# Converting an output weight among the background work of an earlier stage, and storing seven block parts in pairs

## The chip, the cores and the metric

The kernel runs on one core of a Trainium2 chip. The metric is device time in microseconds (us) of one execution; lower is better. Work goes to TensorE (PE: matmuls; PEld: its weight loads), VectorE (DVE), ScalarE (ACT) and GpSimd (POOL). Every transfer between HBM and on-chip memory is issued by one queue on SyncE (SP).

## What is computed

Three blocks follow one another, for 4 batches of 768 tokens: a gated linear attention, a token and channel mixing block, and a gated feed-forward block.

```python
for t in range(S):                                   # attention, 8 heads of 48
    state = f[:, :, t, :, None] * state + einsum('bhd,bhe->bhde', k[:, :, t], v[:, :, t])
    y[:, :, t] = einsum('bhd,bhde->bhe', q[:, :, t], state)
theta = x @ w_theta                                  # mixing, x is (4, 768, 384)
y = einsum('ts,bsd->btd', w_tok_r, x * cos(theta)) + einsum('ts,bsd->btd', w_tok_i, x * sin(theta))
u = x + y
x = u + maximum(u @ w_ch, 0)
h = maximum(x @ w_in, 0)                             # feed-forward, d_ff 1024
u, v = h[..., :512], h[..., 512:]
v_n = (v - mean(v)) / sqrt(var(v) + 1e-6)
v_s = einsum('ts,bsd->btd', w_spatial, v_n) + b_spatial[None, :, None]
out = (u * v_s) @ w_out                              # w_out is (512, 384)
```

## The kernel before

The program has two stages. **Stage 1** is the attention and the mixing block of all batches, **stage 2** the feed-forward block, batch by batch.

In stage 1 PE does the attention's small products (`psc`, `pw`, `px`), the theta products (`pth`), the token mix (`acc`, 36 groups of matmuls a half batch, which read the token weights `tk` and the rotated inputs `z`), and the channel product (`hh`), which reads `uT`. `uT` is made by ACT and DVE from a finished `acc` (`p1_u`). The token weights come back from HBM for every half batch as pairs of 384 KB transfers (`tk<-tkp`) into three buffers each.

Matmuls run in a rounded format. For full accuracy an operand x is split into hi and lo (`split`): ACT writes hi, DVE writes lo = x - hi, and `mm3` does three matmuls for one product. A weight that arrives in float64 (`w_in`, `w_out`) is first made into float32 by `single`: one transfer into a staging buffer `ws` (two of them), one ACT pass, three DVE passes into `wb`. `weight` is `single` followed by `split`.

The order of instructions of stage 1 is not the order of the code. A planner (`Plan`) records every instruction with an assumed cost, runs a list scheduler over the five engines for four rounds, and pins the best order that it found on each engine. Some work of stage 2 is handed to the planner as background work, from the tick `WTICK` on and with a due time that lies `IDLE` later than the end: the conversion of `w_in` (`w2_load`, into `wi`), the split of the first batch's inputs (`p2_x`, into `x2`), and the blocks of the spatial weight (`w_blocks`). The pools `a1` and `a2` of the attention are closed before; tiles that take their place are held back by `Plan.after`.

`w_blocks` prepares what a seven-product scheme for v_s needs. For each of three row tiles s it loads two tiles of `w_spatial` into `wr`, forms four differences in `wt`, splits `wr` and `wt` as two pieces of 128x1536 through one buffer `wz` (the low part is written over its source), and stores hi and lo to HBM in `wpd0` and `wpd1`. `wr`, `wt` and `wz` exist once each, so a piece waits until the piece before has been stored.

Stage 2 does for each batch: `p2_v` (`pv`, normalised into `vr`), `p2_b` (sums of quarters of v, split into `vn`), `p2_u` (`pu`), `p2_f` (seven products `pg` with the stored blocks, read back by `p2_load` into `sp`; each is finished into the gated values `gt` by `gate`, on DVE and ACT), and `p2_o` (`po` = gt times `wo`). For batch 0 only, `p2_wo` converts `w_out` between `p2_u` and `p2_f`, four tiles of 128x384, one `weight` each.

Every instruction is recorded by one helper, so the profile gives L370 as its line; the tile names tell the places apart.

## Time and profile before

| | |
|---|---|
| median of 3 runs | 627.47 us (624.61 to 629.4) |
| profiled execution, its own time | 624.12 us |
| its span in the trace | 622.3 us |
| mean granted clock of TensorE | 0.977 of full speed |
| busy: PE, DVE, ACT, POOL | 589.8, 457.2, 333.4, 22.3 us |
| moved by DMA | 147.75 MB, 237 GB/s over the span |

Stage 1 lasts from 0 to about 372 us of the span, stage 2 from there to the end, a little under 60 us a batch in the later batches. All times of the trace are us from the start of its span. The profiled execution is a little faster than the runs that were timed.

### The profile page before, as it was taken

The numbers are of one execution on the slowest core, as the hardware profiler recorded it, in microseconds if no ns is written. First come the engines' busy times: TensorE is split into PE (matmuls) and PEld (weight loads), VectorE is DVE, ScalarE is ACT, GpSimd is POOL, SyncE is SP. The second block draws the span as 40 slices with busy tenths as digits, with TensorE's granted clock in tenths as the row PEclk, the third lists the DMA queues.
The fourth block names the chain that finished last, engine by engine and source line by source line (L and its number), as shares of the span: only waits on it lengthen the run. The fifth ranks groups of instructions, "written<-read, shape, count | busy, mean of one in ns | idle before, by whom it ended". The sixth has DMA issues, their size and how long they took to land.

```text
span 622.3 us, 14093 instructions
## 1 busy us (share of the span) xinstructions
PE 589.8 (95%) x5736; PEld 535.7 (86%) x5736; DVE 457.2 (73%) x816; ACT 333.4 (54%) x616; POOL 22.3 (4%) x54
## 2 busy tenths in 40 slices
PE   8678989999999899999999999996999999999995
PEld 8566556776898899989999998996899999999995
DVE  5776889886899649855988457896559766966681
ACT  4556675638967687834875124633453345345421
POOL 4100001000010000000000000000000000000000
PEclk9867999999999999999999999998999999999998
DMA  7798958899688888887989979897109811950332
GB/s 279 204 290 217 278 198 230 292 318 309 226 241 270 279 276 270 246 273 273 348 295 304 374 258 366 292 342 276 40 1 339 306 41 46 360 203 26 116 114 82
DMA packets 65993, 147.75 MB, mean 237 GB/s; under 512 B 6656, under 2 KB 34304, under 8 KB 65920
## 3 DMA queue, kind: packets, MB, share of 16 engines
q1 hardware_dynamic: 65920, 146.77, 70.3%
q8 instruction: 47, 0.77, 0.5%
q14 instruction: 26, 0.21, 0.1%
HBM read 104.20 MB, written 33.03 MB: 221 GB/s over the span
## 4 chain that ended last, share of the span: by engine, by line
PE 70%; DVE 10%; DMA 9%; ACT 4%; issue 3%; SPq 2%; POOL 0%; DVEq 0%; ACTq 0%
PE acc L370 20%; PE pg L370 11%; PE po L370 7%; PE pv L370 6%; PE pu L370 6%; PE hh L370 5%; PE pth L370 5%; PE psc L370 4%; PE px L370 3%; DMA ws<-wo_dram 3%; PE pt L370 2%; SPq L370 2%; PE pw L370 2%; DMA qp<-q 2%; DVE tk L370 2%
## 5 line engine op out<-in xcount | busy, mean ns | idle before, releaser
L370 PE MATMUL acc<-tk,z 128*128 128x384 f32 x792 | 171.9, 368 | 2.6 <-DVE tk L370 2.0
L370 PEld LDWEIGHTS acc<-tk,z 128*128 128x128 f32 x792 | 137.9, 188 | 20.0 <-DVE tk L370 3.1
L370 PE MATMUL pg<-sp,vn 128*128 128x384 f32 x504 | 88.0, 336 | 0.0
L370 PEld LDWEIGHTS pg<-sp,vn 128*128 128x128 f32 x504 | 87.4, 188 | 0.0
L370 PE MATMUL po<-wo,gt 128*128 128x384 f32 x288 | 52.4, 341 | 4.9 <-ACT gt L370 4.9
L370 PEld LDWEIGHTS po<-wo,gt 128*128 128x128 f32 x288 | 50.8, 191 | 5.6 <-ACT gt L370 5.2
L370 PE MATMUL pv<-wi,x 128*128 128x512 f32 x216 | 51.0, 393 | 0.0
L370 PE MATMUL pu<-x,wi 128*128 128x384 f32 x288 | 50.7, 335 | 0.0
L370 PEld LDWEIGHTS pu<-x,wi 128*128 128x128 f32 x288 | 50.1, 188 | 0.3
L370 PEld LDWEIGHTS pv<-wi,x 128*128 128x128 f32 x216 | 41.0, 190 | 8.3
L370 PE MATMUL hh<-uT,wc 128*128 128x384 f32 x216 | 42.0, 342 | 0.2 <-DVE uT L370 0.2
L370 PEld LDWEIGHTS hh<-uT,wc 128*128 128x128 f32 x216 | 37.6, 188 | 1.4 <-DVE uT L370 1.0
L370 DVE BATCH_NORM_STATS2 st<-vr 128x6 f32<-128x512 f32 x24 | 16.6, 691 | 27.7 <-ACT vr L370 27.7
L370 ACT ACTIVATE gt<-g 128x384 fp32r<-128x384 f32 x32 | 16.6, 523 | 37.6 <-DVE g L370 37.5
L370 PE MATMUL psc<-qp,kp 64*64 64x64 f32 x768 | 30.2, 225 | 6.9 <-issue 2.8
L370 DVE TENSOR_TENSOR vn<-vr,vn 128x768 fp32r<-128x768 f32 x24 | 22.9, 956 | 18.4 <-ACT vn L370 17.7
L370 PEld LDWEIGHTS psc<-qp,kp 64*64 64x64 f32 x768 | 27.0, 139 | 9.9 <-issue 5.8
L370 PE MATMUL px<-vc,sc 64*64 64x48 f32 x768 | 29.8, 232 | 3.8 <-issue 3.8
L370 DVE TENSOR_TENSOR sc<-psc,mask 128x384 f32<-128x384 f32 x32 | 17.0, 548 | 21.4 <-PE psc L370 21.3
L370 ACT ACTIVATE ws<-ws 128x768 f32<-128x768 f32 (+2 forms) x28 | 20.8, 744 | 21.7 <-DMA ws<-tok_dram 12.1
L370 PEld LDWEIGHTS px<-vc,sc 64*64 64x64 f32 x768 | 27.4, 151 | 4.2 <-issue 4.1
L370 ACT ACTIVATE vn<-vr 128x768 fp32r<-128x768 f32 x24 | 20.2, 844 | 14.4 <-PE pg L370 14.1
(124 smaller groups left out, 1012.1 us busy)
## 6 DMA issues: line engine op xcount, KB each, us to landing
sp<-wpd SPq DMA_DIRECT2D x56, 576.0 KB, 6.7
tk<-tkp SPq DMA_DIRECT2D x48, 384.0 KB, 4.9
ws<-tok_dram SPq DMA_DIRECT2D x12, 768.0 KB, 6.3
tkp<-tk SPq DMA_DIRECT2D x24, 384.0 KB, 4.8
f<-f_dram SPq DMA_DIRECT2D x12, 384.0 KB, 5.5
k<-k_dram SPq DMA_DIRECT2D x12, 384.0 KB, 5.6
q<-q_dram SPq DMA_DIRECT2D x12, 384.0 KB, 5.7
vn<-vu_dram SPq DMA_DIRECT2D x16, 288.0 KB, 6.1
```

The source lines that it names most:

```text
L370: r = f(*a, **k)
```

## The change

`w_out` is no longer converted in stage 2. Its four `weight` steps become the last steps of `w_blocks`, among the background work that the planner places in stage 1; `wo` moves into the pool `w2`, which lives through both stages, with its first use held back behind the attention's tiles like that of `wi`. The staging buffers of these steps are those of stage 1.

To make room, `w_blocks` gets by with less: the two tiles of `w_spatial` are loaded into the first four rows of the activation buffer `X[0]` (`X0`), which the batches 0 and 2 used before; the hi buffer is double, one in rows 4 and 5 of `X0` and one in `wz`; `wt` has three rows; one difference is formed in place. The eighth block part, B12, which no product reads, is not made nor stored. The seven others are split and stored in pieces of two (the last of one): per row tile four pieces, eight stores, where there were two pieces, four stores.

```diff
-STORED = ["B11", "B12", "B21", "B22", "T1", "T2", "T3", "T4"]
+STORED = ["B11", "T1", "B21", "B22", "T3", "T2", "T4"]
...
     def w2_open(self, ctx):
...
         self.x2 = [w2.tile([P, NJ, S], F32R, name=f"x2{i}") for i in range(2)]
+        self.wo = [w2.tile([P, NF, DM], F32R, name=f"wo{i}") for i in range(2)]
...
     def p2_open(self, ctx):
...
-        self.wo = [d1.tile([P, NF, DM], F32R, name=f"wo{i}") for i in range(2)]
...
-    def w_blocks(self, pool, e):
+    def w_blocks(self, pool, e, X):
         V, sub = self.V, ALU.subtract
+        r, z = X[:, 0:4], [X[:, 4:6].bitcast(F32R), e.tile([P, 2, TH], F32R, name="wz")]
+        t = e.tile([P, 3, TH], F32, name="wt")
+        self.free(z[1])
+        self.free(t)
+        n = 0
         for s in range(3):
-            r, t = [e.tile([P, 4, TH], F32, name=f"w{x}", tag=f"w{x}") for x in "rt"]
-            self.free(r)
-            self.free(t)
...
-            V.tensor_tensor(t[:, 0], r[:, 1], r[:, 0], op=sub)
-            V.tensor_tensor(t[:, 1], r[:, 3], t[:, 0], op=sub)
-            V.tensor_tensor(t[:, 2], r[:, 3], r[:, 1], op=sub)
-            V.tensor_tensor(t[:, 3], r[:, 2], t[:, 1], op=sub)
+            V.tensor_tensor(t[:, 0], r[:, 3], r[:, 1], op=sub)
+            V.tensor_tensor(r[:, 1], r[:, 1], r[:, 0], op=sub)
+            V.tensor_tensor(t[:, 1], r[:, 3], r[:, 1], op=sub)
+            V.tensor_tensor(t[:, 2], r[:, 2], t[:, 1], op=sub)
             yield
-            for i, x in enumerate((r, t)):
-                z = e.tile([P, 4, TH], F32R, name="wz", tag="wz")
-                self.free(z)
-                lo = x.bitcast(F32R)
-                self.split(z, lo, x)
-                for k, y in enumerate((z, lo)):
-                    self.Q.dma_start(out=self.store[k][:, s, 4 * i : 4 * i + 4], in_=y.bitcast(F32))
+            for i, x in ((0, r[:, 0:2]), (2, r[:, 2:4]), (4, t[:, 0:2]), (6, t[:, 2:3])):
+                m = min(2, 7 - i)
+                hi, lo = z[n % 2][:, 0:m], x.bitcast(F32R)
+                n += 1
+                self.split(hi, lo, x)
+                for k, y in enumerate((hi, lo)):
+                    self.Q.dma_start(out=self.store[k][:, s, i : i + m], in_=y.bitcast(F32))
                 yield
+        for f in range(NF):
+            self.weight(self.wo[0][:, f], self.wo[1][:, f], self.a["wo"][P * f : P * f + P, :], pool)
+            yield
...
-            self.plan.after(self.wi + self.x2, ("a1.", "a2."))
+            self.plan.after(self.wi + self.x2 + self.wo, ("a1.", "a2."))
...
-            hold["w"] = self.w_blocks(self.c2, self.e)
+            hold["w"] = self.w_blocks(self.c2, self.pool(se, "e", 1, side="left"), X[B % 2])
...
-        for k in range(3 * 4 + 1):
+        for k in range(3 * 6 + NF + 1):
             at(2 * n * (B - 1) + WTICK + k, block)
...
-        self.store = [dr.tile([P, NT // 2, 8, TH], F32, name=f"wpd{i}") for i in range(2)]
+        self.store = [dr.tile([P, NT // 2, 7, TH], F32, name=f"wpd{i}") for i in range(2)]
...
-            if b == 0:
-                run(self.p2_wo(o))
-                so.close()
```

Because the planner's input changes, its whole order does. Three places matter below. In the names, `xt` and `uT` with the numbers 3810 and 3962 belong to the two halves of batch 3 in stage 1, a number behind `ws`, `wb` or `sp` tells one buffer's use from the next, and `wo0`, `wo1` are the hi and lo parts of `w_out`.

**DVE, first half of batch 3 in stage 1, where `uT` is made from `acc`.** Before:

```order
L370 TENSOR_TENSOR xt_3810<-acc_4165,xt_3810 128x384
L370 TENSOR_SCALAR wb_4525<-ws_4526 128x512
L370 TENSOR_TENSOR xt_3810<-acc_4166,xt_3810 128x384
L370 TENSOR_TENSOR uT1_4370<-xt_3810,uT0_4369 128x384
L370 TENSOR_TENSOR xt_3810<-acc_4167,xt_3810 128x384
L370 TENSOR_TENSOR uT1_4370<-xt_3810,uT0_4369 128x384
L370 SCALAR_TENSOR_TENSOR wb_4525<-ws_4526,wb_4525 128x512
L370 TENSOR_TENSOR uT1_4370<-xt_3810,uT0_4369 128x384
L370 SCALAR_TENSOR_TENSOR wb_4525<-ws_4526,wb_4525 128x512
```

Now:

```order
L370 TENSOR_SCALAR wb_4702<-ws_4703 128x384
L370 SCALAR_TENSOR_TENSOR wb_4702<-ws_4703,wb_4702 128x384
L370 TENSOR_TENSOR X0_129<-X0_129 128x768
L370 SCALAR_TENSOR_TENSOR wb_4702<-ws_4703,wb_4702 128x384
L370 TENSOR_TENSOR xt_3810<-acc_4165,xt_3810 128x384
L370 TENSOR_TENSOR wo1_4249<-wb_4702,wo0_4248 128x384
L370 TENSOR_TENSOR xt_3810<-acc_4166,xt_3810 128x384
L370 TENSOR_TENSOR uT1_4372<-xt_3810,uT0_4371 128x384
L370 TENSOR_TENSOR xt_3810<-acc_4167,xt_3810 128x384
L370 TENSOR_TENSOR uT1_4372<-xt_3810,uT0_4371 128x384
L370 TENSOR_TENSOR wt_4599<-X0_129,wt_4599 128x384
L370 TENSOR_TENSOR uT1_4372<-xt_3810,uT0_4371 128x384
```

The last conversion of `w_in` stood between these steps; now the first conversion of `w_out`, a difference and a low part of the blocks do.

**ACT at the same place.** Before:

```order
L370 ACTIVATE ws_4526<-ws_4526 128x512
L370 ACTIVATE x20_4246<-xs_4589 128x768
L370 ACTIVATE wi0_4244<-wb_4482 128x512
L370 ACTIVATE uT0_4369<-xt_3810 128x384 x3
L370 ACTIVATE wi0_4244<-wb_4525 128x512
L370 ACTIVATE wz_4663<-wt_4651 128x1536
L370 ACTIVATE uT0_4570<-xt_3962 128x384 x3
```

Now:

```order
L370 ACTIVATE wi0_4244<-wb_4527 128x512
L370 ACTIVATE wz_4598<-X0_129 128x768
L370 ACTIVATE X0_129<-X0_129 128x768
L370 ACTIVATE ws_4712<-ws_4712 128x384
L370 ACTIVATE wo0_4248<-wb_4702 128x384
L370 ACTIVATE uT0_4371<-xt_3810 128x384 x3
L370 ACTIVATE wo0_4248<-wb_4711 128x384
L370 ACTIVATE X0_129<-wt_4599 128x768
```

Ahead of the three `uT` steps ACT now has two steps of `w_out`, the first of which waits for the second transfer of `w_out`.

**ACT at the end of stage 1 and the start of stage 2 (`vr<-pv` is the first eviction of stage 2).** Before:

```order
L370 ACTIVATE wz_4663<-wt_4651 128x1536
L370 ACTIVATE uT0_4570<-xt_3962 128x384 x3
L370 ACTIVATE wz_4676<-wr_4668 128x1536
L370 ACTIVATE wz_4681<-wt_4669 128x1536
L370 ACTIVATE vr_4704<-pv_4752 128x512
```

Now:

```order
L370 ACTIVATE wz_4598<-wt_4599 128x384
L370 ACTIVATE uT0_4572<-xt_3962 128x384 x3
L370 ACTIVATE wz_4598<-X0_129 128x768
L370 ACTIVATE X0_129<-X0_129 128x768
L370 ACTIVATE ws_4721<-ws_4721 128x384
L370 ACTIVATE ws_4730<-ws_4730 128x384
L370 ACTIVATE wz_4598<-wt_4599 128x384
L370 ACTIVATE X0_129<-wt_4599 128x768
L370 ACTIVATE wo0_4248<-wb_4720 128x384
L370 ACTIVATE vr_4754<-pv_4799 128x512
L370 ACTIVATE vr_4754<-pv_4822 128x512
L370 ACTIVATE wo0_4248<-wb_4729 128x384
```

Between the last `uT` and the first eviction stood two passes over the blocks; now there are four shorter ones, two passes over staged rows of `w_out` and one hi part.

**DVE in stage 2, batch 0, around the first gates (`g<-pg` is the start of a gate).** Before:

```order
L370 SCALAR_TENSOR_TENSOR wb_5020<-ws_5021,wb_5020 128x384
L370 TENSOR_TENSOR vn1_4907<-s3_4898,vn0_4906 128x768
L370 TENSOR_TENSOR wo1_4699<-wb_5020,wo0_4698 128x384
L370 TENSOR_SCALAR wb_5029<-ws_5030 128x384
L370 SCALAR_TENSOR_TENSOR wb_5029<-ws_5030,wb_5029 128x384 x2
L370 TENSOR_TENSOR vn1_4912<-vr_4704,vn0_4911 128x768
L370 TENSOR_TENSOR g_5092<-pg_5072,kp_5068 128x384
L370 TENSOR_TENSOR wo1_4699<-wb_5029,wo0_4698 128x384
L370 TENSOR_TENSOR g_5092<-g_5092,bs_4700 128x384
L370 TENSOR_TENSOR g_5098<-pg_5082,kp_5069 128x384
L370 TENSOR_SCALAR wb_5038<-ws_5039 128x384
L370 TENSOR_TENSOR g_5092<-g_5092,u2_4705 128x384
```

Now:

```order
L370 TENSOR_TENSOR vn1_4950<-vr_4754,vn0_4949 128x768
L370 TENSOR_TENSOR vn1_4954<-s3_4945,vn0_4953 128x768
L370 TENSOR_TENSOR vn1_4959<-vr_4754,vn0_4958 128x768
L370 TENSOR_TENSOR g_5102<-pg_5082,kp_5078 128x384
L370 TENSOR_TENSOR g_5102<-g_5102,bs_4750 128x384
L370 TENSOR_TENSOR g_5102<-g_5102,u2_4755 128x384
L370 TENSOR_TENSOR g_5108<-pg_5092,kp_5079 128x384
L370 TENSOR_TENSOR vn1_4963<-vr_4754,vn0_4962 128x768
L370 TENSOR_TENSOR g_5108<-g_5108,bs_4750 128x384
```

The `wb` and `wo` steps between the gates are gone, and no other steps came in their place.

## Rows read from the trace of the kernel before

**Rows 1.** The page: busy time, share of the span and instructions of each engine.

```profile
PE 589.8 (95%) x5736; PEld 535.7 (86%) x5736; DVE 457.2 (73%) x816; ACT 333.4 (54%) x616; POOL 22.3 (4%) x54
```

**Rows 2.** Windows: stretch, its length, busy PE PEld DVE ACT POOL, clock, DMA share, GB/s.

```profile
50.00:290.00 240.00, 231.41 (x3162) 190.22 (x3157) 185.50 (x271) 160.56 (x286) 12.77 (x26) 0.99 0.83 264
290.00:350.00 60.00, 60.00 (x353) 59.82 (x352) 51.68 (x85) 39.53 (x68) 0.10 (x1) 1.00 0.92 318
350.00:372.00 22.00, 21.75 (x123) 21.00 (x122) 8.35 (x15) 4.56 (x5) 0.00 (x0) 1.00 0.82 303
396.90:418.70 21.80, 21.80 (x127) 21.80 (x127) 20.01 (x37) 11.09 (x21) 0.00 (x0) 1.00 0.85 293
463.00:484.80 21.80, 21.80 (x127) 21.80 (x126) 16.88 (x30) 8.10 (x13) 0.00 (x0) 1.00 0.82 287
```

**Rows 3.** Timeline of PE, 415 to 512: start, length, what, [idle before, releaser].

```profile
418.73 6.44 PE L370 MATMUL po<-wo,gt 128*128 128x384 f32 x36
430.07 2.29 PE L370 MATMUL po<-wo,gt 128*128 128x384 f32 x6 [4.91 <-ACT gt L370]
...
450.29 12.67 PE L370 MATMUL pu<-x,wi 128*128 128x384 f32 x72
...
484.64 7.46 PE L370 MATMUL po<-wo,gt 128*128 128x384 f32 x42
...
509.49 2.79 PE L370 MATMUL pu<-x,wi 128*128 128x384 f32 x15
```

**Rows 4.** Instructions on the tile wb: count, ns min/median/max, first and last start.

```profile
L370 DVE SCALAR_TENSOR_TENSOR wb<-ws,wb x26: 551/560/694, 48.5 to 412.6; 128x384 uint32<-128x384 uint32 x14, 128x512 uint32<-128x512 uint32 x12
...
L370 DVE TENSOR_SCALAR wb<-ws x13: 352/361/428, 47.4 to 408.2; 128x384 uint32<-128x384 uint32 x7, 128x512 uint32<-128x512 uint32 x6
...
L370 ACT ACTIVATE wo<-wb x4: 518/524/527, 394.1 to 413.2; 128x384 fp32r<-128x384 f32 x4
L370 DVE TENSOR_TENSOR wo<-wb,wo x4: 548/556/559, 394.7 to 417.1; 128x384 fp32r<-128x384 f32 x4
```

**Rows 5.** Instructions on the tile ws: the ACT pass over staged rows.

```profile
L370 ACT ACTIVATE ws<-ws x28: 539/680/980, 31.1 to 404.1; 128x768 f32<-128x768 f32 x12, 128x384 f32<-128x384 f32 x10, 128x512 f32<-128x512 f32 x6
```

**Rows 6.** Instructions on the tile wz: the DVE pass of a split of the blocks.

```profile
L370 DVE TENSOR_TENSOR wr<-wr,wz x3: 1752/1753/1759, 306.3 to 372.2; 128x1536 fp32r<-128x1536 f32 x3
```

**Rows 7.** Timeline of PE, 325 to 372: the last halves of stage 1.

```profile
330.46 15.79 PE L370 MATMUL acc<-tk,z 128*128 128x384 f32 x90
346.09 3.34 PE L370 MATMUL hh<-uT,wc 128*128 128x384 f32 x18
...
367.82 4.46 PE L370 MATMUL hh<-uT,wc 128*128 128x384 f32 x23 [0.25 <-DVE uT L370]
```

**Rows 8.** Timeline of the SP queue, 285 to 432: one pair of token weights.

```profile
333.62 0.80 SPq L370 DMA_DIRECT2D tk<-tkp  x2
```

**Rows 9.** DMA issues, 285 to 402: count, KB each, median us to landing.

```profile
tk<-tkp SPq DMA_DIRECT2D x30, 384.0 KB, 5.2
...
wpd<-wz SPq DMA_DIRECT2D x6, 768.0 KB, 6.3
...
ws<-wo_dram SPq DMA_DIRECT2D x4, 384.0 KB, 7.6
```

**Rows 10.** Timeline of ACT, 350 to 432: last block pass, first eviction of stage 2.

```profile
374.96 1.49 ACT L370 ACTIVATE wz<-wt 128x1536 fp32r<-128x1536 f32 x1 [3.39 <-DMA wpd<-wz]
376.36 0.58 ACT L370 ACTIVATE vr<-pv 128x512 f32<-128x512 f32 x1
```

**Rows 11.** Timeline of DVE, 376 to 400: first statistics, second vn of batch 0.

```profile
378.16 0.69 DVE L370 BATCH_NORM_STATS2 st<-vr 128x6 f32<-128x512 f32 x1
...
396.00 0.95 DVE L370 TENSOR_TENSOR vn<-vr,vn 128x768 fp32r<-128x768 f32 x1
```

**Rows 12.** Timeline of PE, 385 to 410: the start of batch 0's seven products.

```profile
396.89 13.33 PE L370 MATMUL pg<-sp,vn 128*128 128x384 f32 x76
```

More of the change, by code (lines that the diff above doesn't have):

```diff
@@ L428, in split, with single @@
         self.V.tensor_tensor(lo, src if src2 is None else src2, hi.bitcast(F32), op=ALU.subtract)
-    def single(self, out, src, pool, most=2 * TH):
+    def single(self, out, src, pool):
         if src.dtype == F32:
@@ L435, in single @@
         n, b = out.free_size(), out.bitcast(U32)
-        s = pool.tile([P, most, 2], U32, name="ws", tag="ws")[:, 0:n]
+        s = pool.tile([P, 2 * TH, 2], U32, name="ws", tag="ws")[:, 0:n]
         self.Q.dma_start(out=s.rearrange("p n w -> p (n w)"), in_=src.bitcast(U32))
@@ L443, in single, with weight @@
         V.scalar_tensor_tensor(b, s[:, :, 0], 29, b, op0=ALU.logical_shift_right, op1=ALU.bitwise_or)
-    def weight(self, hi, lo, src, pool, most=2 * TH):
-        t = pool.tile([P, most], F32, name="wb", tag="wb", bufs=1)[:, 0 : hi.free_size()]
-        self.single(t, src, pool, most)
+    def weight(self, hi, lo, src, pool):
+        t = pool.tile([P, 2 * TH], F32, name="wb", tag="wb", bufs=1)[:, 0 : hi.free_size()]
+        self.single(t, src, pool)
         self.split(hi, lo, t)
@@ L838, in p2_w @@
             yield
-        yield from self.p2_wo(pool)
-    def p2_wo(self, pool):
         for f in range(NF):
-            self.weight(self.wo[0][:, f], self.wo[1][:, f], self.a["wo"][P * f : P * f + P, :], pool, DM)
+            self.weight(self.wo[0][:, f], self.wo[1][:, f], self.a["wo"][P * f : P * f + P, :], pool)
             yield
-    def w_blocks(self, pool, e):
+    def w_blocks(self, pool, e, X):
         V, sub = self.V, ALU.subtract
+        r, z = X[:, 0:4], [X[:, 4:6].bitcast(F32R), e.tile([P, 2, TH], F32R, name="wz")]
[3 more added lines that the diff above has]
+        n = 0
         for s in range(3):
-            r, t = [e.tile([P, 4, TH], F32, name=f"w{x}", tag=f"w{x}") for x in "rt"]
-            self.free(r)
-            self.free(t)
             for k in range(2):
@@ L855, in w_blocks @@
             yield
-            V.tensor_tensor(t[:, 0], r[:, 1], r[:, 0], op=sub)
-            V.tensor_tensor(t[:, 1], r[:, 3], t[:, 0], op=sub)
-            V.tensor_tensor(t[:, 2], r[:, 3], r[:, 1], op=sub)
-            V.tensor_tensor(t[:, 3], r[:, 2], t[:, 1], op=sub)
+            V.tensor_tensor(t[:, 0], r[:, 3], r[:, 1], op=sub)
+            V.tensor_tensor(r[:, 1], r[:, 1], r[:, 0], op=sub)
+            V.tensor_tensor(t[:, 1], r[:, 3], r[:, 1], op=sub)
+            V.tensor_tensor(t[:, 2], r[:, 2], t[:, 1], op=sub)
             yield
-            for i, x in enumerate((r, t)):
-                z = e.tile([P, 4, TH], F32R, name="wz", tag="wz")
-                self.free(z)
-                lo = x.bitcast(F32R)
-                self.split(z, lo, x)
-                for k, y in enumerate((z, lo)):
-                    self.Q.dma_start(out=self.store[k][:, s, 4 * i : 4 * i + 4], in_=y.bitcast(F32))
+            for i, x in ((0, r[:, 0:2]), (2, r[:, 2:4]), (4, t[:, 0:2]), (6, t[:, 2:3])):
[5 more added lines that the diff above has]
+                    self.Q.dma_start(out=self.store[k][:, s, i : i + m], in_=y.bitcast(F32))
                 yield
+        for f in range(NF):
+            self.weight(self.wo[0][:, f], self.wo[1][:, f], self.a["wo"][P * f : P * f + P, :], pool)
+            yield
     def free(self, t):
@@ L1184, in blocks @@
         def blocks():
-            self.e = self.pool(se, "e", 1, side="left")
-            hold["w"] = self.w_blocks(self.c2, self.e)
+            hold["w"] = self.w_blocks(self.c2, self.pool(se, "e", 1, side="left"), X[B % 2])
         def block():
@@ L1251, in run @@
         f = e.enter_context(tc.tile_pool(name="f", bufs=1, side="left", reuse_waits="tile"))
-        so = ExitStack()
-        o = so.enter_context(tc.tile_pool(name="o", bufs=2, side="right", reuse_waits="tile"))
         self.sp = {}
```

## The prediction

> **What bounds the kernel now.** I read the page first: PE is busy 589.8 us, 95% of the span [rows 1]. So a change can only pay where PE waits or runs at a lower clock. The windows say where that is [rows 2]. From 290 to 350 PE has no idle time at all (60.00 of 60.00), while DVE is busy 51.7 and the DMA engines 92%; from 350 to 372 PE is busy 21.75 of 22.00. From 50 to 290 PE is idle 240.00 - 231.41 = 8.6 us, in attention work that the change doesn't touch by itself. In stage 2 PE is dense but for one place, which the timeline of PE shows [rows 3]: in batch 0, between the output products `po`, PE waits 4.91 us for `gt` from ACT. The reader should look at the same stretch one batch later, where no wait stands.
>
> The size of that loss is best read as a stretch against its twin. From the first `po` of a batch to the first `pu` of the next, the work is 72 `po` and 54 `pv`. In batch 0 it runs from 418.73 to 450.29, 31.56 us; in batch 1 from 484.64 to 509.49, 24.85 us [rows 3]. The difference is 6.7 us. It is more than the wait itself, because the six `po` after it take 2.29 us where 36 took 6.44 us, 0.38 us each against 0.18.
>
> Why the wait is there: in the stretch of the seven products, DVE is busy 20.0 of 21.8 us in batch 0 and 16.9 of 21.8 in batch 1 [rows 2]. The gates run on DVE, and in batch 0 the conversion of `w_out` stands between them.
>
> **The change, part by part.** *Removed from stage 2.* One row tile of `w_out` costs DVE one pass of 0.35 us, two of 0.56 and one of 0.56, 2.0 us; four of them 8.1 us [rows 4]. On ACT it is 0.54 at least and 0.52, so 1.06, or 4.3 us for the four [rows 4, 5]. Some 6 us of the DVE part lies between 396.9 and 418.7, since the four low parts start from 394.7 to 417.1 [rows 4], one of them before that stretch. Taken out, DVE is busy about 14 of 21.8 us there, less than in batch 1, where nothing waits. What is late next is PE itself, and I take the twin: 24.85 instead of 31.56, a gain of **6.7 us**. Bounds: 4.9 if the slow matmuls after the wait stay for another reason, and 6.7 at most, since after it stage 2 has no idle PE to give back.
>
> *Added to stage 1.* The same 8.1 us of DVE and 4.3 us of ACT. DVE is idle 60.00 - 51.68 = 8.3 us from 290 to 350 and 22.00 - 8.35 = 13.7 us from 350 to 372 [rows 2]; the attention's tiles hold `wo` back until near 290. So the work fits into 22 us of idle DVE time, and by throughput it costs nothing. What it costs is a matter of what it stands in front of.
>
> First place, the `uT` of the first half of batch 3. In the old order one conversion step or two stood among them; the number of DVE steps between the first `xt` and the last `uT` is nearly the same in the new order, so DVE itself adds nothing. But ACT now has the staging pass of the second tile of `w_out` ahead of the three `uT` steps, and that pass waits for its transfer. In the queue that transfer stands behind the pair of `tk` that went out at 333.62 [rows 8] and behind one input load, so about 336. These transfers of `w_out` took 7.6 us in the old place, and the `tk` of this stretch 5.2 [rows 9]. It lands between 341 and 344. From there two ACT passes, then the interlaced `xt` and `uT` steps of DVE, some 4.5 us, end at 346 to 348. PE starts the `hh` that needs them at 346.09 [rows 7], and needs the last one about a microsecond later. I take a wait of 0.5 us, from 0 to 3.
>
> Second place, the `uT` of the last half. PE waited 0.25 us for them at 367.82 [rows 7], so nothing covers a delay. The new order puts one difference of the blocks (a DVE pass of 0.56, as the 384 wide pass of [rows 4]) ahead of the last of the three. That is **0.5 us** on PE's path if the load behind the difference has landed, which is issued after the last `tk` as before, but now with shorter stores ahead of it. From 0 to 2.
>
> Third place, the change of stages. ACT's first eviction of `pv` came at 376.36, after a block pass that had waited 3.39 us for a store [rows 10]. The new order puts four block passes, two staging passes and a hi part ahead of it, and DVE's first statistics come after the low part of the last tile. I expect the eviction some 1 us later and the statistics about 3 us later than 378.16 [rows 11]. The cover: the products start at 396.89 [rows 12] and want the second `vn` one product later, at 396.89 + 21.8/7 = 400.0, while it was ready at 396.95 [rows 11]. That is 3 us of cover, to which the 2.0 us of the first `w_out` tile come back that DVE did before 396. I charge nothing, from 0 to 2.
>
> *The blocks.* A low part of 1,536 elements takes DVE 1.75 us [rows 6], one of 384 takes 0.56 [rows 4]; by the line through the two one of 768 takes 0.95. Per row tile that is 3 x 0.95 + 0.56 = 3.4 us against 2 x 1.75 = 3.5. So the passes are a wash, and with two hi buffers a piece no longer waits for the store before it. The stores double in number, from 12 to 24, and four loads join them, so 16 more transfers pass the SP queue; in bytes, 1.2 MB of stores go and 1.6 MB of loads come, 0.4 MB or 1.3 us at the 318 GB/s of that stretch [rows 2]. These bytes lie beside PE as long as `tk` comes in time: a `tk` buffer is used again after three steps, so a transfer has two steps of 15.79/5 = 3.16 us, 6.3 us in all [rows 7], against 5.2 [rows 9]. The cover is 1.1 us. I charge nothing.
>
> The trace shows that half as large a transfer isn't half as long: 384 KB land after 5.2 us, 768 KB after 6.3 [rows 9], with many in flight. The Trainium skill speaks against this part: its page DMA: Bandwidth & Descriptors (section Anatomy of one DMA) gives each transfer 2.0 us and its bytes at 436 GB/s, and (section Bandwidth) advises batches of 1 MiB or more. By its fit, as an estimate, 768 KB take 3.8 us, 384 KB 2.9 and 192 KB 2.5, so the stores would take 18 x 2.9 + 6 x 2.5 = 67 us instead of 46. If the queue worked them off one by one that would be 21 us more; its fixed part was taken on another issue path, and no run here shows transfers one by one.
>
> *Stage 1 before 290.* The planner is run anew, and even the first steps stand otherwise. Nothing says in which direction. The idle time there, 8.6 us, is the most that a better order could give, and a worse one could cost as much. I take 0 and 2.5 us to either side.
>
> **The sum.** 6.7 - 0.5 - 0.5 = 5.7 us less: the profiled execution would go from 624.12 to 618.4. The median of the runs lies 627.47 - 624.12 = 3.35 us above that execution; carried over, 621.8 us. A change of 1%, 6.3 us, is about what a measurement of this kernel tells from none, so the likeliest outcome lies just inside it.
>
> **The rivals.**
>
> *The order gives more.* Stage 1 loses some of its 8.6 us of idle PE besides. For it: the search starts from other numbers and keeps its best. Against: it did so before too. With 4 us more the time is 618.
>
> *The wait moves to stage 1.* The second `w_out` transfer lands late and ACT stands before `uT`, 3 us; the last difference waits for its load, 2 us. Together 5 of the 6.7 us go, and it ends near 626. For it: 92% busy DMA engines and ACT's fixed order. Against: ACT had idle time ahead of `uT`.
>
> *Slower: `tk` comes late.* Sixteen more transfers push each pair of `tk` behind others. The price decides at a landing of 6.3 us: each of the 10 steps of the last two halves then waits for the excess. At 7.6 us, what the `w_out` transfers took in the same queue, that is 10 x 1.3 = 13 us, against a gain of 5.7: 627.5 + 7.3 = 635 us. Break-even with the kernel before is at 6.9 us. Against: the bytes hardly grow, and 30 `tk` have a median of 5.2. The rule of the Trainium skill on small transfers (DMA: Bandwidth & Descriptors, section Bandwidth) stands behind this rival: by its fit, as an estimate, the stores alone would take 21 us more.
>
> *The change does nothing.* Batch 0 still waits for `gt`, because the later start of the statistics makes the gates as late as `w_out` did. Then 0 to -1 us are left, 627.5. Against: DVE gets 8.1 us back and starts 3 late.
>
> **How the numbers follow.** The forecast with its spread of 2.5 us, 619 to 624.5: chance 0.54. More from the order, 615 to 619: 0.15. The wait moves, 624.5 to 629: 0.18. Nothing: 0.05. Slower, 630 to 640: 0.08. The range 616 to 629 leaves out the slow rival and about a third of the second case. Faster by over 1% means below 621.2: the second case and 0.45 of the first, 0.15 + 0.24 = 0.39. Slower by over 1% means above 633.7: 0.06. The rest is 0.55.
>
> **What would show it.** The wait of `po` for `gt` in batch 0 is gone, and its stretch from `po` to `pu` takes about 24.9 us: the main term. DVE is busy about 14 us in the products of batch 0. PE's idle time before the two last groups of `hh` in stage 1 is about 0.5 us each. `tk` still lands in under 6.3 us, and no `acc` after 290 waits. PE's idle time from 50 to 290 is within 2.5 us of 8.6. The forecast is wrong if stage 1 ends more than 3 us away from where it ended, or if a wait of `pg` for `vn` or `sp` appears in batch 0.

## The result, and the profile after

The changed kernel takes 619.15 us (median of four runs, 617.89 to 621.44) against 627.63 for the kernel before (four runs, 624.61 to 629.40): a ratio of 0.987, 95% interval 0.983 to 0.992. The forecast was 621.8. The profiled execution took 619.71 us, its span is 617.9. Here and below a median is that of all runs of a kernel, while a ratio leaves out the slow ones, over 1.5% above the fastest of their kernel.

The page's busy times, to be held against [rows 1]:

```profile
PE 589.9 (95%) x5736; PEld 534.2 (86%) x5736; DVE 457.7 (74%) x822; ACT 332.0 (54%) x622; POOL 21.3 (3%) x54
```

No engine's busy time moved by more than 1.4 us, so what changed is mainly when the work is done. The windows of the first four stretches of [rows 2] (the last is that of batch 0's products):

```profile
50.00:290.00 240.00, 233.10 (x3154) 191.23 (x3147) 188.51 (x277) 162.54 (x292) 10.79 (x26) 0.99 0.83 265
290.00:350.00 60.00, 60.00 (x349) 59.74 (x349) 53.45 (x91) 38.21 (x68) 0.10 (x1) 1.00 0.96 334
350.00:372.00 22.00, 20.11 (x109) 18.34 (x108) 7.13 (x15) 4.88 (x8) 0.00 (x0) 1.00 0.83 290
398.10:420.00 21.90, 21.90 (x129) 21.90 (x128) 17.89 (x32) 8.72 (x15) 0.00 (x0) 1.00 0.82 289
```

The timeline of PE in stage 2, against [rows 3]:

```profile
419.96 7.79 PE L370 MATMUL po<-wo,gt 128*128 128x384 f32 x42
...
445.18 12.67 PE L370 MATMUL pu<-x,wi 128*128 128x384 f32 x72
...
479.52 7.55 PE L370 MATMUL po<-wo,gt 128*128 128x384 f32 x42
...
504.54 10.76 PE L370 MATMUL pu<-x,wi 128*128 128x384 f32 x61
```

The wait for `gt` is gone. From the first `po` of batch 0 to the next `pu` (called the stretch below) it is 445.18 - 419.96 = 25.22 us, 6.34 less than in [rows 3] and about the same as batch 1's 504.54 - 479.52 = 25.02. The end of stage 1, against [rows 7]:

```profile
344.74 3.34 PE L370 MATMUL hh<-uT,wc 128*128 128x384 f32 x18
...
363.27 3.22 PE L370 MATMUL acc<-tk,z 128*128 128x384 f32 x17 [0.57 <-DMA tk<-tkp]
...
367.60 3.13 PE L370 MATMUL hh<-uT,wc 128*128 128x384 f32 x14 [0.25 <-DVE uT L370]
371.64 1.85 PE L370 MATMUL hh<-uT,wc 128*128 128x384 f32 x9 [0.91 <-DVE xt L370]
```

PE reached the `hh` of the first half 1.35 us earlier than before (344.74 against 346.09 in [rows 7]) and lost it again behind: stage 1 ends, with the first `pv`, at 373.34, where it was 372.12. The DMA issues from 285 to 402 (number, KB each, median us to landing), against [rows 9]:

```profile
tk<-tkp SPq DMA_DIRECT2D x30, 384.0 KB, 5.3
...
wpd<-X SPq DMA_DIRECT2D x12, 384.0 KB, 5.0
...
ws<-wo_dram SPq DMA_DIRECT2D x4, 384.0 KB, 6.9
wpd<-wz SPq DMA_DIRECT2D x3, 384.0 KB, 3.8
wpd<-wt SPq DMA_DIRECT2D x3, 384.0 KB, 5.7
wpd<-wz SPq DMA_DIRECT2D x3, 192.0 KB, 5.6
```

### The profile page after: what moved, and what is told of

The parts are those of the page before. It is cut to its first block, busy times and chain, and to the rows that moved or that the text cites. A ratio compares the mean times of both kernels' runs of the same rounds, so it can differ in the third digit from the quotient of the medians.

```text
span 617.9 us, 14127 instructions
## 1 busy us (share of the span) xinstructions
PE 589.9 (95%) x5736; PEld 534.2 (86%) x5736; DVE 457.7 (74%) x822; ACT 332.0 (54%) x622; POOL 21.3 (3%) x54
## 4 chain that ended last, share of the span: by engine, by line
PE 83%; DVE 6%; DMA 5%; issue 2%; ACT 2%; POOL 0%; SPq 0%; DVEq 0%; ACTq 0%
PE acc L370 21%; PE pg L370 14%; PE pu L370 8%; PE pv L370 8%; PE po L370 8%; PE hh L370 6%; PE pth L370 6%; PE px L370 4%; PE psc L370 4%; PE pt L370 3%; DMA kp<-k 2%; PE pw L370 2%; DVE tk L370 2%; DVE icp L370 1%; DMA wpd<-wt 1%
## 5 line engine op out<-in xcount | busy, mean ns | idle before, releaser
L370 PE MATMUL acc<-tk,z 128*128 128x384 f32 x792 | 174.3, 369 | 1.8 <-DVE tk L370 1.2
L370 PE MATMUL pth<-ft,xt 128*128 128x384 f32 x72 | 25.5, 493 | 0.6 <-ACT xt L370 0.6
```

What stands on the lines that cost most here:

```text
L370: r = f(*a, **k)
```

## The experiments

My first theory was the prediction's: 8.1 us of DVE passes over `w_out` stand among the gates of batch 0, and taking them out removes the wait. Its rival was that the transfers of `w_out` come late, and that the lateness makes the wait. This table sums up what follows. The passes are those of DVE from the first `pv` on; the column beside them adds up those that start after the first product `pg`. The wait is batch 0's. All these are from the profiled executions, in us; the ratio to the kernel before is from runs.

| kernel | passes in stage 2 | behind the first `pg` | wait of `po` for `gt` | stretch | ratio, 95% interval |
|---|---|---|---|---|---|
| before, three profiles | 16, data late | 6.1, 6.1, 6.1 | 4.91, 4.88, 4.18 | 31.56, 32.41, 31.75 | |
| before, three buffers | 16, data later | 8.2 | 4.98 | 32.78 | 1.002, 0.998 to 1.006 |
| blocks only | 16, data late | 7.8 | 4.18 | 32.07 | 1.000, 0.997 to 1.004 |
| idle passes put back | 8 early, 16 with data from `u` | 3.7 | 2.26 | 27.50 | 0.994, 0.991 to 0.998 |
| no DVE passes | 0, data late | 0 | 0.87 | 25.98 | 0.991, 0.986 to 0.996 |
| loads early | 10, data early | 0 | 0.83 | 25.96 | 0.992, 0.988 to 0.997 |
| no transfers | 16, data early | 0 | none | 25.18 | 0.986, 0.980 to 0.992 |
| changed, two profiles | 8, data early | 0, 0 | none | 25.22, 25.22 | 0.987, 0.983 to 0.992 |

**Passes without transfers, transfers without passes.** Both are edits of the kernel before. In the first the DVE passes are left out:

```diff
-            self.weight(self.wo[0][:, f], self.wo[1][:, f], self.a["wo"][P * f : P * f + P, :], pool, DM)
+            s = pool.tile([P, DM, 2], U32, name="ws", tag="ws")
+            self.Q.dma_start(out=s.rearrange("p n w -> p (n w)"), in_=self.a["wo"][P * f : P * f + P, :].bitcast(U32))
+            for w in self.wo:
+                self.A.activation(w[:, f], s[:, :, 1].bitcast(F32), AF.Copy, scale=REBIAS)
```

> The kernel before with the sixteen DVE passes over w_out in batch 0 left out: the four transfers stay, and two ACT passes a tile write wo straight from the staged rows, so wo and the output are not w_out's. Stage 1 is as before. Theory (the wait of po for gt came from 8.1 us of DVE work between the gates): the wait goes, the stretch of batch 0 from the first po to the next pu takes 25 us instead of 31.6, about 6.5 us less in all. Rival (the four late transfers of w_out, for which ACT waits in order, held the gates up): the wait stays within 1.5 us of 4.9 and the time within 2 us of before.

In the second the four transfers are replaced by fills on GpSimd, and all passes stay:

```diff
-        self.Q.dma_start(out=s.rearrange("p n w -> p (n w)"), in_=src.bitcast(U32))
+        if fill:
+            self.G.memset(s.rearrange("p n w -> p (n w)").bitcast(F32), 1.0)
+        else:
+            self.Q.dma_start(out=s.rearrange("p n w -> p (n w)"), in_=src.bitcast(U32))
```

> The kernel before without the four transfers of w_out in batch 0: GpSimd fills the staging buffers with a constant, all ACT and DVE passes stay (wo and the output are not w_out's). Stage 1 is as before. Theory (DVE's passes make the wait): the wait of po for gt stays, 3 to 5 us, since DVE has the same 8.1 us to do; it may shrink by up to 2 us where the passes move into DVE's free time before the products. Rival (the late transfers make it): the wait goes, 25 us from po to pu, 6.5 us less.

The first took 623.47 us, the second 618.27, where the kernel before took 627.99 on the same chip. Each edit alone nearly empties the stretch of its wait. PE's timeline without the DVE passes:

```profile
431.77 1.31 PE L370 MATMUL po<-wo,gt 128*128 128x384 f32 x6 [0.87 <-ACT gt L370]
```

The first theory, as a matter of the amount of work, doesn't survive the second edit: all sixteen passes are there, at their place in the program text, and PE waits for nothing. PE's timeline without the transfers:

```profile
425.17 7.82 PE L370 MATMUL po<-wo,gt 128*128 128x384 f32 x42
432.82 4.27 PE L370 MATMUL pv<-wi,x 128*128 128x512 f32 x18
...
450.35 4.87 PE L370 MATMUL pu<-x,wi 128*128 128x384 f32 x27
```

What changed is where the passes run. Without the transfers they run from 386.6 to 403.8; the last of them starts just ahead of the first product, which starts at 403.33, and the gates follow later (the lines are that pass and the first step of the gates, from DVE's timeline):

```profile
403.24 0.56 DVE L370 TENSOR_TENSOR wo<-wb,wo 128x384 fp32r<-128x384 f32 x1
...
410.04 0.55 DVE L370 TENSOR_TENSOR g<-pg,kp 128x384 f32<-128x384 f32 x1
```

In the second profile of the kernel before they run from 396.2 to 421.6, and the products start at 400.90.

The windows show what that does to DVE (the third busy time). They follow stage 2's parts: `pv`, `pu`, the first 10 us of the seven products `pg`, the rest of them, and 12.4 us from the first `po`. The kernel before, second profile:

```profile
376.13:388.39 12.26, 12.26 (x55) 10.14 (x55) 8.54 (x24) 4.29 (x10) 0.00 (x0) 1.00 0.96 357
388.39:400.90 12.51, 12.51 (x73) 12.50 (x72) 11.33 (x34) 7.12 (x19) 0.00 (x0) 1.00 1.06 382
400.90:410.90 10.00, 10.00 (x59) 10.00 (x59) 8.39 (x15) 7.50 (x15) 0.00 (x0) 1.00 0.60 193
410.90:422.73 11.83, 11.83 (x70) 11.83 (x69) 11.83 (x23) 3.74 (x7) 0.00 (x0) 1.00 1.06 376
422.73:435.13 12.40, 7.52 (x40) 7.21 (x40) 12.06 (x25) 4.59 (x9) 0.00 (x0) 0.89 1.02 366
```

The same five without the transfers:

```profile
378.56:390.82 12.26, 12.26 (x56) 10.14 (x55) 9.41 (x25) 6.05 (x13) 0.74 (x1) 1.00 1.01 359
390.82:403.33 12.51, 12.51 (x74) 12.51 (x72) 12.47 (x44) 7.96 (x21) 0.74 (x1) 1.00 0.92 328
403.33:413.33 10.00, 10.00 (x59) 10.00 (x59) 9.88 (x14) 6.76 (x12) 0.00 (x0) 1.00 0.52 184
413.33:425.16 11.83, 11.83 (x70) 11.83 (x69) 11.80 (x24) 4.12 (x7) 0.00 (x0) 1.00 1.03 371
425.16:437.56 12.40, 12.32 (x65) 11.27 (x65) 8.83 (x19) 4.79 (x10) 0.00 (x0) 1.00 0.84 301
```

Over the whole length DVE works as much in both, 52.2 us (8.54 + 11.33 + 8.39 + 11.83 + 12.06) and 52.4. But when the first `po` starts, it has done 40.1 us of it in the kernel before and 43.6 without the transfers. The 3.5 us of difference is idle time that DVE had earlier, and could not use because the rows of `w_out` were not there: ACT's first pass over them starts at 395.61, after waiting 1.58 us for the transfer. The longest such wait of DVE behind the first product stands in the second profile of before, first in ACT's timeline, then in DVE's:

```profile
408.10 0.55 ACT L370 ACTIVATE ws<-ws 128x384 f32<-128x384 f32 x1 [1.77 <-DMA ws<-wo_dram]
408.55 0.83 ACT L370 ACTIVATE vn<-vr 128x768 fp32r<-128x768 f32 x1
```

```profile
409.42 0.96 DVE L370 TENSOR_TENSOR vn<-vr,vn 128x768 fp32r<-128x768 f32 x1 [1.30 <-ACT vn L370]
410.29 0.55 DVE L370 TENSOR_TENSOR g<-pg,kp 128x384 f32<-128x384 f32 x1
```

ACT's queue stands at the last transfer with `vn` behind it; DVE stands at `vn` with the first step of the gates behind it. That step starts 410.29 - 400.90 = 9.4 us after the first product; without the transfers it is 6.7 us, and in the changed kernel 403.02 - 398.12 = 4.9 us. DVE's line in the changed kernel:

```profile
403.02 0.55 DVE L370 TENSOR_TENSOR g<-pg,kp 128x384 f32<-128x384 f32 x1
```

In the kernel before DVE has no idle time left from there to catch up in, and the gates end late. ACT's staging passes wait like this without the DVE passes too: there the last four end at 408.1, the `vn` behind them starts at 408.39, DVE waits for it, and the first gate starts 7.5 us after the first product. This is probably why 0.87 us are left; it wasn't tried by itself.

```profile
409.28 0.96 DVE L370 TENSOR_TENSOR vn<-vr,vn 128x768 fp32r<-128x768 f32 x1 [3.31 <-ACT vn L370]
```

Two things are bound together in these runs. The rows land late, and the order of DVE's steps, which is the same in all three profiles of the kernel before, puts passes behind the first product. Every edit that takes the transfers away or makes them early changes that order too. No run has the old order with early rows, so how much each of the two does by itself is not shown.

**The passes put back without transfers.** The changed kernel, with sixteen idle DVE passes of the same kinds, 8.1 us, ahead of the gates of batch 0; they read `u`, which ACT writes during `pu` and `pg`:

```diff
+    def extra(self, pool):
+        V, y = self.V, pool.tile([P, TH], F32, name="y", tag="y", bufs=1)
+        for f, th in ((0, 0), (3, 0), (1, 1), (3, 1)):
+            x = self.u2[:, f, TH * th : TH * th + TH]
+            V.tensor_scalar(y, x, 0.5, None, op0=ALU.mult)
+            V.scalar_tensor_tensor(y, x, 0.5, y, op0=ALU.mult, op1=ALU.add)
+            V.scalar_tensor_tensor(y, x, 0.5, y, op0=ALU.mult, op1=ALU.add)
+            V.tensor_tensor(y, x, y, op=ALU.subtract)
...
+            if b == 0:
+                self.extra(f)
```

> The changed kernel with sixteen idle DVE passes of the same sizes (8.1 us) put back between p2_u and p2_f of batch 0, reading u and writing a scratch tile; no transfer, no ACT pass; stage 1 is that of the changed kernel. Theory: the wait of po for gt comes back, 3 to 5 us, the stretch from po to pu takes 29 to 32 us, the kernel is 4 to 7 us slower than the changed one. Rival (transfers or ACT were the cause): within 1.5 us of the changed kernel, 25 us for the stretch.

It took 623.04 us, about 4 more than the changed kernel, and the stretch is 27.50:

```profile
423.77 6.50 PE L370 MATMUL po<-wo,gt 128*128 128x384 f32 x36
432.53 1.32 PE L370 MATMUL po<-wo,gt 128*128 128x384 f32 x6 [2.26 <-ACT gt L370]
...
451.27 4.00 PE L370 MATMUL pu<-x,wi 128*128 128x384 f32 x22
```

So passes that stand there from 393 to 416 us cost 2.3 us of the stretch, a third of the 6.3 to 7.2 that the kernel before loses there. That lies between the two cases of the expectation: the theory had 29 to 32 us, its rival 25. Of the 8.1 us of idle passes only 3.7 start after the first product.

**The transfers early, the passes where they were.** The changed kernel, with the raw rows of `w_out` loaded in stage 1 and kept, and the conversion back in stage 2:

```diff
-        self.wo = [w2.tile([P, NF, DM], F32R, name=f"wo{i}") for i in range(2)]
+        self.wr = [w2.tile([P, DM, 2], U32, name=f"wr{f}") for f in range(NF)]
...
-            self.weight(self.wo[0][:, f], self.wo[1][:, f], self.a["wo"][P * f : P * f + P, :], pool)
+            self.Q.dma_start(out=self.wr[f].rearrange("p n w -> p (n w)"), in_=self.a["wo"][P * f : P * f + P, :].bitcast(U32))
...
+    def p2_wo(self):
+        for f in range(NF):
+            t = self.w2.tile([P, S], F32, name="xs", tag="xs", bufs=2)[:, 0:DM]
+            self.single(t, self.a["wo"], None, self.wr[f])
+            self.split(self.wo[0][:, f], self.wo[1][:, f], t)
...
+            if b == 0:
+                self.p2_wo()
```

> The changed kernel, but only the four transfers of w_out stay in stage 1 (into four raw tiles of their own, among the background work); the conversion itself, 16 VectorE and 8 ScalarE passes, is back in stage 2, written where the kernel before has it, and the two result tiles are stage 2's again. Theory (late transfers: before, the passes fall among the gates only because their data lands late): the passes find their data at once and run ahead of the gates, TensorE's wait for a gate is under 1 us, and from the first block of the output product to the next batch's first product it is 25 to 26.5 us (32 with the late transfers, 25.2 in the changed kernel); time 618 to 621. Rival (the amount of VectorE work in stage 2): the wait for a gate stays at 2 us or more, that stretch is 27 us or more, time 622 to 625, as with the 16 idle passes put back. A second rival: the early passes hold up the statistics and with them the spatial products, which then start 1 to 3 us later after the last product of v than in the changed kernel, with no wait for a gate.

The test is weaker than meant: the compiled order moved six of the sixteen passes into stage 1, and the other ten ran from 381.6 to 390.6, ahead of `pg`. None stands among the gates any more. The wait is 0.83 us and the stretch 449.83 - 423.87 = 25.96, as the theory of the late transfers had it:

```profile
423.87 6.41 PE L370 MATMUL po<-wo,gt 128*128 128x384 f32 x36
431.11 1.32 PE L370 MATMUL po<-wo,gt 128*128 128x384 f32 x6 [0.83 <-ACT gt L370]
...
449.83 12.67 PE L370 MATMUL pu<-x,wi 128*128 128x384 f32 x72
```

What is left of the wait doesn't come from the passes. The first gate starts 4.9 us after the first product, as in the changed kernel. The difference is the split of batch 1's inputs among the last gates, for whose load (`xs<-x2d`) ACT waited 2.71 us here, and DVE for ACT. DVE's line in this run, then in the changed kernel:

```profile
424.56 0.96 DVE L370 TENSOR_TENSOR x<-xs,x 128x768 fp32r<-128x768 f32 x1 [1.66 <-ACT x L370]
...
419.87 0.96 DVE L370 TENSOR_TENSOR x<-xs,x 128x768 fp32r<-128x768 f32 x1 [0.87 <-ACT x L370]
```

The extra 1.66 - 0.87 = 0.79 us is about the 0.74 by which the stretch is longer than the changed kernel's. The second rival of the expectation is out too: from the first `pv` to the first `pg` it is 24.8 us in both kernels.

The time, 623.69, is not as the theory had it, and 3.5 us more than the changed kernel took on the same chip (620.18). This execution's stage 1 ended at 377.24, with a wait of 2.06 us that the background work makes there:

```profile
375.55 1.85 PE L370 MATMUL hh<-uT,wc 128*128 128x384 f32 x9 [2.06 <-DVE xt L370]
377.24 12.45 PE L370 MATMUL pv<-wi,x 128*128 128x512 f32 x54
```

From the first `pv` to the end it took 621.9 - 377.24 = 244.7 us, and the changed kernel's two profiles 244.6 and 244.4: stage 2 is as quick with the conversion in it as without. Whether stage 1 is slower for good in this kernel, or this is its spread (see below), isn't settled.

**The transfers later still.** The kernel before, with one number changed:

```diff
-        o = so.enter_context(tc.tile_pool(name="o", bufs=2, side="right", reuse_waits="tile"))
+        o = so.enter_context(tc.tile_pool(name="o", bufs=3, side="right", reuse_waits="tile"))
```

> The kernel before with three staging buffers for w_out in stage 2 where it has two. The space of the third comes free later, and in the compiled order all four transfers then stand together behind the spatial loads that they were spread among, and the first conversion pass stands behind the four earliest vn steps instead of ahead of them. The same 16 VectorE passes and the same bytes, only later. Theory (lateness of the data makes the wait): the wait for a gate in batch 0 is no shorter than before, 4.9 us, and rather longer, up to 7; the stretch from the first output product to the next batch's first product is 32 to 35 us; time 627 to 631. Rival (the number of staging buffers, or the amount of VectorE work): with three buffers the last transfers start sooner after the first, the wait shrinks below 4 us, the stretch to 30 us or less, 624 to 627.

All four transfers were issued from 388.0 to 402.1 instead of 382.6 to 401.2, and the passes ran from 400.1 to 424.0 instead of 392.0 to 417.6. The stretch is the longest of all, but hardly longer than before's 32.41:

```profile
430.98 2.29 PE L370 MATMUL po<-wo,gt 128*128 128x384 f32 x6 [4.98 <-ACT gt L370]
...
452.37 12.67 PE L370 MATMUL pu<-x,wi 128*128 128x384 f32 x72
```

More buffers didn't help, against the rival; the wait didn't grow either, though the passes are 6 to 8 us later and PE's stage only 1 us. In this run, with 8.2 us of passes behind the first product instead of 6.1, it mattered little where exactly they fell.

**The blocks alone.** The changed kernel, with `w_out` converted in stage 2 again, as before:

```diff
+            if b == 0:
+                run(self.p2_wo(o))
+                so.close()
...
-        for f in range(NF):
-            self.weight(self.wo[0][:, f], self.wo[1][:, f], self.a["wo"][P * f : P * f + P, :], pool)
-            yield
```

> The changed kernel with w_out converted in stage 2 of batch 0 again, as before; the blocks are prepared in the new way (staged in X0, two hi buffers, pairs, seven parts). Theory (the gain is the conversion's move; the blocks are about neutral): the wait of po for gt is back at 4 to 5 us, the stretch from po to pu at 31 to 32 us, and the time is within 4 us of before. Rival (the gain comes from the blocks or the new order of stage 1): faster than before by 5 us or more, with the wait present.

It took 627.65 us, a ratio of 1.000 with an interval of 0.4%, or 2.5 us, to either side, and the wait is back. So seven block parts stored in pairs and rows staged in an X buffer are worth nothing that shows by themselves, and the gain comes with the move of `w_out`. The order of stage 1 is not held fixed by this: the planner's input is a third one here, and so is its order.

**How far two profiles agree.** The kernel before was run twice more and the changed kernel once, for their profiles.

> The kernel before itself, for a second profile of it (its first one was an execution of 624.1 us, 3.4 below the median of its runs, while the two profiles of the changed kernel lie within 1.3 us of theirs). If the first profile was one of its quick executions, this one ends stage 1 later (first product of v at 374 to 379 us instead of 372.1) with the same 31.6 us from the first output product to the next batch's first product, and the difference of 8.5 us between the medians is 6.3 us of stage 2 and some 2 us of stage 1. If it agrees with the first within 1 us, then the difference of the medians that the profiles do not show (some 4 us) is not in stage 1, and stays open.

> The same kernel once more, for a third profile: the same two cases as for the second. Rival to both: the 31.6 us stretch itself differs by more than 1 us between executions of the kernel before, and the 6.3 us are not a fixed price.

> The changed kernel itself once more, for the comparison with the others on one chip and for a second profile. Its time should be 618 to 621. If the part of stage 1 up to 290 us, where the program is nearly the same, differs between the two profiles by more than 1 us, then differences of that size between profiles there are spread and not the change; if it agrees within 0.5 us, they are the change.

The runs of the kernel before had a median of 626.61 beside 628.25, those of the changed one 620.18 beside 628.93, a ratio of 0.987 again (0.979 to 0.995). The stretch is steady, as the table shows; the end of stage 1 is not. With the stage 1 of the kernel before, unedited, it came at 372.12, 376.13 and 373.18, and in the three edits of that kernel at 377.88 (no DVE passes), 378.56 (no transfers) and 372.98 (three buffers). With that of the changed kernel it came at 373.34, 372.84 and, with the idle passes, 377.16. The means are 375.1 and 374.4. So the first profile of before lies 3.0 us under the mean of its stage 1, which is the first case of its expectation, in part; and any difference between the two orders of stage 1 is hidden in a spread of 6.4. The waits in the tail spread too. The last group of 90 `acc` began at 329.04 and 330.71 us in the two profiles of the changed kernel, so differences of 1.7 us there are spread, and in the second only one wait of the tail is left, 0.25 us of `hh` for `uT` at 368.09.

**Other orders of the background work.** Three tries at something better, all on the changed kernel. First, `w_out` ahead of the blocks:

```diff
         n = 0
+        for f in range(NF):
+            self.weight(self.wo[0][:, f], self.wo[1][:, f], self.a["wo"][P * f : P * f + P, :], pool)
+            yield
         for s in range(3):
```

> The changed kernel with the four w_out conversions ahead of the spatial blocks in the background work, nothing else. Theory (stage 1's tail in the changed kernel loses 2.6 us after 345 us to late background work, its VectorE waiting 1.0 us for a store of wt): the order moves that work but does not shrink it, and the stores of the blocks move later; between 617 and 622 beside the changed kernel's 619 to 620, stage 2 unchanged (25 us from the first output product to the next batch). Rival: the last stores of the blocks come so late that the first loads of stage 2 are late, TensorE then waits for sp ahead of the spatial products, 622 or more.

Then `w_out` at the end of the loading of the first weight, and the same with a smaller required gap:

```diff
-        for k in range(2 * NJ + 1):
+        for k in range(2 * NJ + NF + 1):
...
-WTICK, IDLE = 37, 25
+WTICK, IDLE = 37, 10
```

> The changed kernel with the four w_out conversions at the end of the steady loading of the first weight of stage 2, one each five places of the order and without the required gap for background work. Theory: the same work, some of it 10 to 20 us earlier, where the DMA engines are as full (0.92 to 0.96 of their time): 617 to 622, and a wait for tk of 0.5 to 2 us in stage 1. Rival: less work is left in the last 30 us, the 2.6 us that stage 1's tail loses come back: 616 to 618.

> The kernel with the w_out conversions at the end of the loading of the first weight, and the required gap for background work cut from 25 to 10. Theory (background work fills gaps of its engines, a smaller required gap moves it earlier and leaves the last 30 us of stage 1 freer): 616 to 619. Rival (with DMA at 0.92 to 0.99 of its time there, earlier stores only delay the tk loads): waits for tk of 1 us or more between 290 and 372 us, 620 to 623.

They took 621.25, 619.57 and 621.71 us, ratios of 0.988 (0.983 to 0.992), 0.986 (0.979 to 0.993) and 0.991 (0.986 to 0.995). The stretch is 25.2 to 25.3 in all three. None is told apart from the changed kernel. The first two came out inside their expected ranges. The last has the time of its rival, but not its reason: after 290 no `acc` waits for `tk` in its profile, nor in the other two, and no `pg` waits for `sp` in the first.

## Why the prediction came out as it did

*The main term* was 6.7 us, 24.85 instead of 31.56 in the stretch. It measured 6.34 between the two first profiles, and 31.91 - 25.22 = 6.7 between the means of all. Taking the twin stretch of batch 1 as the measure, rather than the wait of 4.91, was right, and it gave the size without the reason. All the rest of stage 2 stood still: from the `pu` behind the stretch to the end it is 172.0, 172.9 and 172.9 us before, 172.7 and 172.5 after.

*Its reason* was half right. I put the wait down to the amount of DVE work between the gates and forecast DVE at about 14 us in the products of batch 0. It was 17.89. The step that failed is the subtraction: 20.0 less 6 supposes that what is left stays where it was. It doesn't, because DVE was full to the end of the products and work had been pushed out behind them; in the 12.4 us from the first `po` on it was busy 12.06 (second profile before), and 8.8 in the changed kernel. What moved out made room for what had been late. The cause, as far as the experiments go, is that the rows came late and the passes, and ACT's staging passes in front of `vn`, fell into the one place without slack, behind the first product. The same passes on early data and ahead of that place cost nothing that shows in the stretch, and even the changed kernel has half of its sixteen in stage 2: in both its profiles they run from 373.7 to 380.4, beside `pv`, where nothing is late. That moving them helped was thus predicted for a reason that would not have told a reader that in this stage moving the transfers alone is cure enough. For the whole kernel that is not shown, since the run with early loads took 3.5 us more than the changed kernel.

*The first place in stage 1*, 0.5 us at the first `uT`, cost nothing. I had the second transfer of `w_out` land between 341 and 344. ACT's timeline:

```profile
339.76 0.55 ACT L370 ACTIVATE ws<-ws 128x384 f32<-128x384 f32 x1 [2.94 <-DMA ws<-wo_dram]
...
342.75 0.53 ACT L370 ACTIVATE uT<-xt 128x384 fp32r<-128x384 f32 x1 [0.40 <-DVE xt L370]
```

ACT did wait for it, 2.94 us, and had that time: the last of these `uT` passes ended at 343.3, ahead of the `hh` at 344.74.

*The second place*, 0.5 us from 0 to 2, came out near its size by luck. The difference that the prediction named, ahead of the last `uT`, ran at 367.46 and cost nothing: the wait of `hh` for `uT` is 0.25 us in both profiles, as in all three before. One profile has another 0.91, the other none. They come from a later difference, ahead of a step that takes a finished `hh` (`xt<-hh`), and what held it up was not the load but a store: it waited for the store that last read `wt`, of which there is one buffer. The line of DVE's timeline:

```profile
370.56 0.56 DVE L370 TENSOR_TENSOR wt<-X,wt 128x384 f32<-128x384 f32 x1 [1.02 <-DMA wpd<-wt]
```

*The change of stages* was charged nothing, and took nothing. The first eviction of `pv` came at 376.18, 0.2 us earlier than in [rows 10] (forecast 1 later), the statistics began at 380.27, 2.1 us later than in [rows 11] (forecast about 3), and `pg` follows `pu` without a gap, at 398.12. *The blocks*, a wash: so the ratio of 1.000 says, to within its 2.5 us. That a piece no longer waits for a store was wrong: ACT stood 6.09 us ahead of a `wz` pass at 355.10 for a store of `wz`, in time it had. `tk` landed in 5.3 us, inside the 6.3 that were its cover; still one `acc` waited 0.57 us for it in one of the two profiles, which "no `acc` waits" had ruled out. A median says little of the latest one in thirty. The doubled stores cost nothing that shows: a store of 384 KB landed in 3.8 to 5.7 us among the others where those of 768 KB took 6.3 to 8.4 before. The fit of the Trainium skill (DMA: Bandwidth & Descriptors, section Anatomy of one DMA), applied one by one, had put them, as an estimate, at up to 21 us; the ratio of 1.000 doesn't agree with that.

*The order before 290* was 0 with 2.5 us to either side. PE's idle time from 50 to 290 is 6.9 and 7.9 us in the two profiles after, 8.6, 9.6 and 8.2 before: about 1.4 less, as the rival that the order gives more had it, but not beyond the spread of the three.

*The carry-over.* The forecast lay 2.65 us above the time. That of the profiled execution, 618.4, lay 1.3 us below the 619.71 that it took. Adding 3.35 us to 618.4 is the same as taking 5.7 from the median of before, and that median held: it was 626.6 to 628.9 us in every later set of runs. So it isn't the carrying over that was short, but the gain: 8.5 us between the medians, where the sum had 5.7. Of the 2.8 us, 1.0 are the two charges in stage 1, of which one cost nothing and the other 0.9 us or nothing. The remaining 8.5 - 6.7 = 1.8 us are not settled. They may be stage 1's order, and they are within the noise: the interval of the ratio allows a gain of 5 to 11 us. The spans of the two first profiles alone would have shown 622.3 - 617.9 = 4.4 us, because the first of before was a quick execution. Its two others took 629.85 and 626.16 us, and ended stage 1 4.0 and 1.1 us later.

## What to carry to other kernels

When an engine on the way to a wait is full, ask when its work could have started, not only how much there is: a stretch can be full because its inputs came late and an idle time before it was lost. Four transfers issued among others in a queue were such inputs here, and making them early was worth about as much in that stage as taking away the work. Price a stall by the whole stretch against a twin without the stall. Judge a gain by the medians of many runs and by stretches of several profiles, not by the spans of two profiled executions.

## What was not expected of the hardware

The six matmuls behind the wait ran at half speed, 0.38 us each against 0.18, in all five profiles in which PE had been idle for 4.2 to 5.0 us before them (2.29 us for the six each time), and took 0.22 in the three with 0.8 to 2.3 us of idle time. The granted clock of the 12.4 us from the first `po` agrees: its mean is 0.89 in the second profile of before, so a part was at the lower of the two levels (1.2 and 2.4 GHz), and after the wait of 2.26 us it is 1.00:

```profile
423.76:436.16 12.40, 10.14 (x54) 9.41 (x54) 10.04 (x20) 4.35 (x10) 0.00 (x0) 1.00 0.80 289
```

So the longer wait cost 6 x 0.16 = 1.0 us more than its own length in the six `po`. The lower clock went on behind them: the 16 `pv` took 5.16 us at a mean clock of 0.69, where they took 3.64 at 1.00 after the wait of 2.26, another 1.5 us. In the first profile of before they took 4.26, so 0.6 more. The prediction named only the six `po` for the difference between 4.9 and 6.7. And a store of 192 KB landed no sooner than one of 384 KB: 5.6 against 3.8 from `wz`.
